# A linear-attention and Fourier-mixing kernel on one core: the k·v product with its operands' roles exchanged, more output buffers, and a new hand-written order

## The chip, the core and the metric

The kernel runs on one core of a Trainium2 chip. TensorE (PE in the profile; its weight loads are the row PEld) multiplies and transposes into PSUM, which has eight banks of 128 partitions x 512 FP32. VectorE (DVE), ScalarE (ACT) and GpSimd (POOL) do the rest, and SyncE (SP) issues the transfers between HBM and the core's own memory. Each engine takes its instructions in the order in which the program lists them, and waits at one whose input or buffer isn't ready.

The metric is the device time of one execution in microseconds (us), as the median of several runs.

## What is computed

```python
def phi(x):                                   # x: (4, 4, 1088, 32): batch, head, row, 32
    a = einsum('rd,bhsd->bhsr', S1, x)        # r = 8
    b = einsum('rd,bhsd->bhsr', S2, x)
    return einsum('bhsi,bhsj->bhsij', a, b).reshape(..., 64)

q_p, k_p = phi(q), phi(k)
kv  = einsum('bhsf,bhsd->bhfd', k_p, v)       # 64 x 32 for each batch and head
z   = sum(k_p, axis=2)
att = einsum('bhsf,bhfd->bhsd', q_p, kv) / (einsum('bhsf,bhf->bhs', q_p, z) + 1e-6)

x = att, heads side by side                   # (4, 1088, 128)
u = x + real(fft(fft(x, axis=1), axis=2))
un = (u - mean(u)) / sqrt(var(u) + 1e-6)      # over the 128 columns
out = u + relu(un @ w_ch1) @ w_ch2            # 128 -> 512 -> 128
```

So each of the four batches needs the table kv, one 64 x 32 block for each of its four heads, with z as a 33rd column, before any of its attention rows can be made. Everything behind attention needs all rows of a batch.

## The kernel before, in words

The work is written as Python generators ("chains"), one for each stage and batch. The string `ORDER` (L39 to L48) lists their names, and each name runs that chain to its next `yield`: k0 is one step of the k stage of batch 0. As nothing else schedules, `ORDER` sets the order of every engine's instructions. `BANKS` (L49 to L57) gives the PSUM bank of each accumulator in the order in which they are asked for; an accumulator waits until the bank's last reader is done.

The stages of a batch b, with their lines:

- S and T: constants (L249 to L305: `memset`s on DVE, `iota`s on POOL, ten warming matmuls), the projections `sblk` and `sab` (L310 to L313), and the tables of cosines and sines (`angles`, `turns` on DVE L226 to L235; `sines` on ACT L239, L240; tables derived from them on POOL L330 to L344). T is in two halves: a short one of 448 columns and a long one of 896.
- L: loads (L190 to L218), all issued on SP.
- k (L358): transposes of k (`ptrk`, L365), copies to `kT` (ACT, L368), projections (`pab`, L374), a copy of one factor (ACT, `ak`, L378), the products `kp` (DVE, L382), two instructions of 128x1024. Then the product with v (`pk`, L396): for each head and each of nine row tiles one FP32 matmul, and then the copies `kvt` (L404), one more matmul (`pkv`, L407) and the copies `kvz` (L411).
- v (L453): POOL copies v into `vpad` with a column of ones behind it: [v|1], 33 columns for each head.
- y and w: the ninth row tile of k and of q, which two batches share (L414 to L451).
- q (L461): transposes (`ptrq`, L468), copies `qT` (L471, L473), projections (`pq`, L483), copies `qa` (ACT, L490), products `qpT` (DVE, L497).
- p (L505): `pnd`, the product of `qpT` with `kvz` (L518), the division on DVE (`den`, `rec`, `x`, L525 to L528), then sums of x on POOL (`xw`, `xf`, L541, L543) and copies on ACT.
- z (L551): the first Fourier transform (`pz`, L558 and L565; `pze`, L573 and L577).
- D and M (`chain_u`, L591): u, the two halves of a batch; E the shared ninth tiles. Bank `pu` (L601 to L607), its copy `u` (ACT, L610), statistics (DVE, L615), five small POOL instructions, a square root (ACT, L628) and a reciprocal (DVE, L631).
- d, m and e (`chain_f`, L634): `pT` (L642 to L650), its copy `uT` (ACT, L653), four products `ph` (L658) with ReLUs to `ht`, turn about on ACT (L661) and DVE (L663), the second product `po` (L671), and on DVE `ot` = po · rstd + u (L679). SP sends `ot` out (L684; L691 in four pieces for e). For the last batch `po` and its output are cut in two.

In `pk` of before, the stationary operand is [v|1] (128 rows x 33 columns) and the moving one is `kp` (128 rows x 64 columns). Two heads, h and h+2, go to PSUM partitions 0 to 32 and 64 to 96. The result is therefore kv transposed, 33 x 64, and `pkv` turns it with an identity. There are 2 x 9 x 2 = 36 such matmuls in a batch, and each leaves two records in the profile, since an FP32 matmul runs as two passes with a weight load of its own each.

Buffers: pool `up` (L110) holds three `u` tiles and three `uT` tiles, `op` (L113) two `ot` tiles. A tile is written anew only when the last reader of the one before in its place is done; for `ot` that reader is the output transfer.

Of the kernel before, what the change touches and what calls it, by code (L numbers as in the profile page):

```python
# [10 lines left out]
FP32 = mybir.dt.float32  # L11
# [11 lines left out]
def _ap(base_ap, p0, nparts, offset_delta, dims):  # L23
    pstep = base_ap.ap[0][0]
    return bass.AP(
        tensor=base_ap.tensor,
        offset=base_ap.offset + p0 * pstep + offset_delta,
        ap=[[pstep, nparts]] + [list(d) for d in dims],
    )


def _back(ap, n):
# [4 lines left out]

WARM = [10]
ORDER = """  # L39
S T T k0 S k0 q0 k0 q0 q0 k0 y0 q0 L q0 k0 y0 v0 y0 q0 q0 k0 q0 k1 k1 L T q0 L k0 k1 k0  # L40
q1 k1 q0 q1 w0 p0 q1 q1 k1 v1 q1 p0 p0 k1 T k1 w0 p0 k2 q2 q1 w0 k2 T k1 w0 q1 q1 p0 q1
p0 v2 k2 p1 q1 k2 q2 y1 k2 W p0 q2 y1 p1 p1 y1 k2 p1 q2 p0 k2 p1 k3 k3 z0 q2 k2 w1 q2 z0
q2 p2 w1 p1 q2 k3 p1 d0 v3 q2 p2 m0 D0 w1 d0 k3 z1 d0 m0 z1 d0 d0 m0 z0 q3 z1 q2 D0 z0
m0 w1 q3 m0 q3 k3 q3 p2 D0 p2 p1 p2 q3 p2 k3 k3 q3 q3 q3 M0 q3 d0 D0 D1 e0 q3 p2 m0 e0
k3 d0 D1 E0 e0 d1 z1 D1 m1 p3 M0 p3 E0 p3 p3 M0 p2 p3 z2 z2 d1 D1 M0 z2 p3 m0 e0 d1 M1
d1 e0 m2 e0 d1 m1 E0 p3 m1 z2 d2 d1 M1 p3 m1 E0 d2 d1 d2 D2 e0 d2 m1 D2 z3 d2 M1 M2 M2
z3 D2 M1 m1 D2 z3 m1 d2 E1 M2 d2 e1 m2 z3 m2 E1 m2 M2 m2 M3 e1 e1 e1 M3 e1 m3 E1 m2 E1
m3 e1 m2 e1 m3 M3 D3 M3 d3 m3 D3 m3 d3 d3 D3 d3 d3 m3 m3 D3 m3 d3 d3 d3  # L48
"""  # L49
BANKS = [  # L50
    0, 1, 2, 3, 4, 5, 6, 7, 0, 1, 2, 3, 4, 6, 7, 0, 3, 5, 4, 1, 2, 4, 1, 5, 6, 7, 4,
    1, 5, 0, 6, 3, 2, 4, 1, 7, 6, 5, 3, 0, 2, 4, 1, 7, 6, 5, 3, 0, 1, 2, 4, 5, 3, 0,
    7, 6, 3, 0, 7, 1, 2, 4, 5, 3, 0, 7, 1, 2, 6, 4, 5, 3, 1, 2, 4, 5, 3, 1, 2, 4, 5,
    3, 1, 2, 5, 4, 3, 0, 1, 7, 2, 5, 4, 3, 6, 5, 0, 1, 4, 3, 7, 2, 6, 5, 0, 4, 1, 7,
    3, 2, 5, 0, 4, 1, 7, 3, 2, 5, 4, 0, 1, 7, 3, 6, 2, 5, 4, 1, 0, 7, 6, 2, 5, 4, 0,
    1, 7, 6, 3, 2, 5, 4, 0, 7, 1, 6, 2, 3, 4, 0, 5, 7, 1, 6, 2, 3, 4, 0, 5, 1, 7, 2,
    6, 3, 0, 4, 5, 1, 7,  # L57
]


# [1 line left out]
def kernel(  # L62
# [44 lines left out]
    qpTp = ctx.enter_context(tc.tile_pool(name="qpTp", bufs=2))  # L107
    xp = ctx.enter_context(tc.tile_pool(name="xp", bufs=2))
    zp = ctx.enter_context(tc.tile_pool(name="zp", bufs=2))
    up = ctx.enter_context(tc.tile_pool(name="up", bufs=3))  # L110
    sp = ctx.enter_context(tc.tile_pool(name="sp", bufs=4))
    hp = ctx.enter_context(tc.tile_pool(name="hp", bufs=2))
    op = ctx.enter_context(tc.tile_pool(name="op", bufs=2))  # L113
    psum = ctx.enter_context(tc.tile_pool(name="psum", bufs=1, space=bass.MemoryType.PSUM))
    banks = iter(BANKS)

    def bank(name):
        return psum.tile([128, 512], FP32, name=name, tag=f"p{next(banks)}")
# [30 lines left out]
    w1_b = const.tile([128, HID], BF16, name="w1_b")  # L149
    w2_b = const.tile([128, 4, 128], BF16, name="w2_b")  # L150
    kvz = [const.tile([128, 2, 2, D + 1], FP32, name=f"kvz{i}") for i in range(2)]
    kvts = [const.tile([128, 2, R * R], FP32, name=f"kvt{i}") for i in range(2)]
    vpads = [const.tile([128, NT, H, D + 1], FP32, name=f"vpad{i}") for i in range(2)]
    zz = [const.tile([128, 2, 512], BF16, name=f"z{i}") for i in range(2)]
    zes = [const.tile([128, 2, 128], BF16, name=f"zE{i}") for i in range(2)]
# [93 lines left out]
    def chain_start():  # L249
        nc.vector.memset(warm_act[:], 0.0)  # L250
        nc.vector.memset(wdummy[:], 0.0)
        nc.scalar.activation(out=warm_act[:, 1:2], in_=warm_act[:, 0:1], func=ACT.Sin)
        loads(0)
        make_identity(nc, ident_f[:])
        def iota(out, pattern, base, mult):
            nc.gpsimd.iota(out, pattern=pattern, base=base, channel_multiplier=mult,
                           allow_small_or_imprecise_dtypes=True)

        iota(s_f[:, 3:4], [[1, 1]], 0, 1)
        iota(kk[:, 0:DM], [[1, DM]], 0, 0)  # L260
        iota(s_f[:, 0:2], [[1, 2]], 1, 2)
        iota(kk[:, DM : DM + E], [[544, 2], [1, 32]], 256, 0)
        iota(kk[:, DM + E : DM + 320], [[1, 2], [2, 128]], 1, 0)
        nc.gpsimd.iota(odd_i[:, :], pattern=[[1, 1]], base=0, channel_multiplier=1)
        iota(s_f[0:64, 2:3], [[1, 1]], 512, 1)
        iota(s_f[64:128, 2:3], [[1, 1]], 1600, 1)
        iota(kk[:, DM + 320 :], [[1, 2], [2, 128]], 545, 0)
        for t_ in kvts:
            nc.vector.memset(t_[:], 0.0)
        for t_ in kvz:  # L270
            nc.vector.memset(t_[:], 0.0)
        nc.vector.memset(bias_halfpi[:], float(np.pi / 2))
        nc.vector.memset(bias_eps[:], 1e-6)
        nc.vector.memset(mask[:], 0.0)
        for h in range(H):
            nc.vector.memset(mask[32 * h : 32 * h + 32, h : h + 1], 1.0)
        for t_ in vpads:
            nc.vector.memset(t_[:, 0:8, :, D : D + 1], 1.0)
        for t_ in qpTes:
            nc.vector.memset(t_[:], 0.0)  # L280
        nc.vector.memset(kk[:, DM : DM + 1], 0.0)
        nc.vector.memset(kk[:, DM + 32 : DM + 33], 544.0)

        nc.vector.tensor_scalar(out=odd_i[:, :], in0=odd_i[:, :], scalar1=1, scalar2=None, op0=AND)
        nc.vector.tensor_copy(par[:, 1:2], odd_i[:, :])
        nc.vector.tensor_scalar(out=par[:, 0:1], in0=par[:, 1:2], scalar1=-1.0, scalar2=1.0,
                                op0=MULT, op1=ADD)
        nc.vector.tensor_scalar(out=s_n[:, 2:3], in0=s_f[:, 2:3], scalar1=par[:, 1:2],
                                scalar2=0.5 / S, op0=SUB, op1=MULT)
        nc.vector.memset(s_n[0:2, 2:3], 0.0)  # L290
        nc.vector.memset(s_n[64:66, 2:3], 0.5)
        for i, t_ in enumerate(vpads):
            nc.vector.tensor_copy(t_[:, 8, :, D : D + 1], _ap(par, 0, 128, i, [[0, H], [0, 1]]))
        nc.vector.tensor_scalar(out=s_n[:, 0:2], in0=s_f[:, 0:2], scalar1=1.0 / S, scalar2=None,
                                op0=MULT)
        nc.vector.tensor_scalar(out=s_n[:, 3:4], in0=s_f[:, 3:4], scalar1=1.0 / DM,
                                scalar2=None, op0=MULT)

        nc.vector.tensor_copy(_ap(sel, 0, 16, 0, [[R, R], [1, R]]),
                              _ap(ident_f, 0, 16, 0, [[1, R], [0, R]]))  # L300
        nc.vector.tensor_copy(_ap(sel, 0, 16, 64, [[R, R], [1, R]]),
                              _ap(ident_f, 0, 16, R, [[0, R], [1, R]]))
        nc.vector.tensor_copy(_ap(sel, 0, 16, 128, [[16, 4], [1, 16]]),
                              _ap(ident_f, 0, 16, 0, [[0, 4], [1, 16]]))
        keep_warm(WARM[0])  # L305
        yield


        ps12 = bank("ps12")
        nc.tensor.matmul(ps12[:, 0:192], s12[:, :, :], sel[:, :, :], start=True, stop=True)  # L310
        nc.vector.tensor_tensor(out=sblk[:, :, :], in0=_ap(ps12, 0, 128, 128, [[16, 4], [1, 16]]),
                                in1=_ap(mask, 0, 128, 0, [[1, 4], [0, 16]]), op=MULT)
        nc.scalar.copy(_ap(sab, 0, 128, 0, [[1, 128]]), ps12[:, 0:128])  # L313
        yield
# [43 lines left out]
    def chain_k(b):  # L358
# [29 lines left out]

        vpad, ep = vpads[b % 2], Y[b // 2]["ep"]
        pk = bank("pk")  # L390
        for hh in range(2):
            for t in range(NT):
                for h in (hh, hh + 2):
                    src = kp[:, h, t, :] if t < 8 else ep[:, h, :]
                    p0 = 64 * (h // 2)
                    nc.tensor.matmul(pk[p0 : p0 + D + 1, 64 * hh : 64 * hh + 64],  # L396
                                     vpad[:, t, h, :], src,
                                     start=(t == 0), stop=(t == NT - 1))
            if hh == 0:
                yield  # L400
        kvt = kvts[b % 2]
        for i in range(2):
            r = slice(64 * i, 64 * i + D + 1)
            nc.scalar.copy(kvt[r, :, :], pk[r, 0:128])  # L404
        yield
        pkv = bank("pkv")
        nc.tensor.matmul(pkv[:, 0 : 2 * (D + 1)], kvt[:, :, :],  # L407
                         _ap(ident_f, 0, 128, 0, [[64, 2], [1, D + 1]]), start=True, stop=True)
        kv = kvz[b % 2]
        for c in range(2):  # L410
            nc.scalar.copy(kv[64 * c : 64 * c + 64, :, c, :],  # L411
                           _ap(pkv, 64 * c, 64, 0, [[D + 1, 2], [1, D + 1]]))

    def last_tile(src):  # L414

# [218 lines left out]
    def chain_f(b, g):  # L634
# [13 lines left out]
        else:  # L648
            for i in range(nt):
                nc.tensor.matmul(pT[:, i * 128 : (i + 1) * 128], A[b]["x"][:, 4 * g + i, :],  # L650
                                 ident_b[:, :], start=False, stop=(i == nt - 1))
        uT = up.tile([128, 512], BF16, name="uT", tag="uT")
        nc.scalar.copy(uT[:, 0:n], _back(pT, n) if g == 1 else pT[:, 0:n])  # L653
        yield
        ht = hp.tile([128, 4, 512], BF16, name="ht", tag="ht")
# [104 lines left out]
```

## Time and profile before

| | |
|---|---|
| median of 3 runs | 91.38 us (91.29 to 91.52) |
| the profiled execution, its own time | 90.52 us |
| its span, first to last instruction | 88.7 us |
| granted TensorE clock | 0.989 |
| PE, PEld busy | 80.2 us, 63.0 us |
| DVE, ACT, POOL busy | 67.7, 62.3, 45.7 us |
| `pk` L396: matmuls, records with kp | 36 in a batch; x256 records in four batches |
| `kvt` copies L404 on ACT | x8, 2.1 us |
| `kvz` copies L411 on ACT | x8, 1.7 us |
| `memset`s of `kvt` L269 on DVE | x2, 0.3 us |
| `ot` L679 on DVE | x34, 9.6 us |

A profile comes from one execution. Its time is 1.8 us above its span, which runs from the first instruction to the last one, and 0.86 us below the median of the runs. "Busy" is the union of an engine's instructions. A matmul's record holds its way through the array as well, so records of matmuls that follow one another overlap: what one matmul costs the engine is the distance from its start to the next one's start, and not the record's length. A row of the chain of waits ("start us, us, what xcount") counts time once, so there the length divided by the number of matmuls is that distance.

### The profile page before, as it was taken

To read this page: it belongs to the slowest core of one execution; us is meant where nothing else is said; L and a number is where in the kernel's file an instruction comes from. 1 tells how busy PE (TensorE), PEld (TensorE's weight loads), DVE (VectorE), ACT (ScalarE), POOL (GpSimd) and SP (SyncE) were. 2 spreads that over 40 slices of the span, in tenths; PEclk is the share of its full clock that TensorE was granted. 3 is DMA by queue.
4 is the path that set the end of the run, shared out by engine and by line. 5 is a ranking of instruction groups with operands and counts; after the bars stand their busy time and mean duration, and the time that the engine had idled before them with its cause. 6 is when DMAs were issued, how large, how long until landed. Compare 5 with 4: busy or idle time off the path is not lost.

```text
span 88.7 us, 3662 instructions
## 1 busy us (share of the span) xinstructions
PE 80.2 (90%) x1481; PEld 63.0 (71%) x1486; DVE 67.7 (76%) x223; ACT 62.3 (70%) x160; POOL 45.7 (52%) x102
## 2 busy tenths in 40 slices
PE   4998979999999999999999999999999999798700
PEld 1366558988979589867776988978767797574500
DVE  5990599998917989419379996959979995999850
ACT  6029657576997597777999897675899967668300
POOL 7200600399242993599502629996599675443000
PEclk9999999999999999999999999999999999999995
DMA  0979888899949760000000000020030313303033
GB/s 21 289 196 277 248 224 194 224 331 282 255 62 275 198 227 0 7 0 0 7 0 0 7 0 11 16 102 7 0 118 0 120 33 124 118 0 128 24 131 106
DMA packets 15124, 9.67 MB, mean 109 GB/s; under 512 B 3972, under 2 KB 14980, under 8 KB 15108
## 3 DMA queue, kind: packets, MB, share of 16 engines
q1 hardware_dynamic: 15028, 9.44, 37.5%
q8 instruction: 11, 0.18, 0.9%
q14 instruction: 5, 0.04, 0.2%
q10 hardware_dynamic: 80, 0.01, 0.1%
HBM read 7.22 MB, written 2.23 MB: 107 GB/s over the span
## 4 chain that ended last, share of the span: by engine, by line
PE 64%; DVE 21%; ACT 4%; DMA 3%; issue 2%; SPq 1%; DVEq 0%; ACTq 0%
PE pnd L518 11%; PE pq L483 10%; PE pk L396 10%; DVE ot L679 6%; DVE ht L663 5%; PE pab L374 5%; DVE stats L615 4%; PE ptrq L468 4%; PE ptrk L365 3%; DMA out_dram<-ot 3%; PE ph L658 3%; PE pz L565 3%; PE po L671 2%; PE pT L650 2%; PE pz L558 2%
## 5 line engine op out<-in xcount | busy, mean ns | idle before, releaser
L497 DVE TENSOR_TENSOR qpT<-qa,pq 128x256 f32<-128x256 f32 x32 | 11.8, 414 | 7.1 <-ACT qa L490 7.1
L541 POOL TENSOR_TENSOR xw<-x 128x512 f32<-128x512 f32 x8 | 10.0, 1274 | 7.4 <-DVE x L528 6.5
L663 DVE TENSOR_SCALAR ht<-ph 128x512 bf16<-128x512 f32 (+1 forms) x20 | 11.5, 600 | 2.7 <-PE ph L658 2.7
L490 ACT COPY qa<-pq 128x256 f32<-128x256 f32 x32 | 9.9, 388 | 4.2 <-PE pq L483 2.2
L455 POOL COPY vpad<-vm 128x1024 f32<-128x1024 f32 x4 | 4.2, 1050 | 15.2 <-DMA vm<-in_v_dram 12.4
L382 DVE TENSOR_TENSOR kp<-ak,pab 128x1024 f32<-128x1024 f32 x8 | 9.6, 1214 | 2.9 <-ACT ak L378 2.9
L658 PE MATMUL ph<-uT,w_b 128*128 128x512 bf16 (+1 forms) x39 | 10.7, 346 | 0.5 <-ACT uT L653 0.2
L679 DVE SCALAR_TENSOR_TENSOR ot<-po,rstd,u 128x128 f32<-128x128 f32 x34 | 9.6, 341 | 1.9 <-DMA out_dram<-ot 1.0
L661 ACT ACTIVATE ht<-ph 128x512 bf16<-128x512 f32 (+1 forms) x20 | 10.5, 542 | 0.6 <-PE ph L658 0.6
L543 POOL TENSOR_TENSOR xf<-xw 128x512 bf16<-128x512 f32 x8 | 10.0, 1277 | 0.3
L671 PE MATMUL po<-w_b,ht 128*128 128x128 bf16 x136 | 9.4, 219 | 0.4 <-ACT ht L661 0.4
L518 PEld LDWEIGHTS pnd<-kvz,qpT 128*64 128x64 f32 x256 | 8.3, 137 | 1.8 <-issue 0.6
L518 PE MATMUL pnd<-kvz,qpT 128*64 128x66 f32 x256 | 9.4, 224 | 0.0
L483 PE MATMUL pq<-qT,sab 32*64 32x256 f32 x256 | 9.0, 387 | 0.0
L671 PEld LDWEIGHTS <-ht 128*128 128x128 bf16 x136 | 8.2, 98 | 1.1 <-ACT ht L661 0.5
L396 PE MATMUL pk<-kp,vpad 128*33 128x64 f32 x256 | 8.5, 219 | 0.1
L396 PEld LDWEIGHTS pk<-kp,vpad 128*33 128x33 f32 x256 | 7.6, 111 | 0.7 <-issue 0.7
L621 POOL TENSOR_TENSOR mv<-stats 128x4 f32<-128x4 f32 (+1 forms) x10 | 2.0, 202 | 11.0 <-DVE stats L615 6.3
L615 DVE BATCH_NORM_STATS2 stats<-u 128x6 f32<-128x128 f32 x34 | 7.5, 278 | 0.0
L528 DVE TENSOR_TENSOR x<-pnd,rec 128x384 f32<-128x384 f32 x12 | 6.7, 557 | 0.6
L610 ACT COPY u<-pu 128x512 f32<-128x512 f32 (+1 forms) x10 | 5.3, 526 | 2.2 <-PE pu L605 0.8
L483 PEld LDWEIGHTS pq<-qT,sab 32*64 32x64 f32 x256 | 4.9, 131 | 2.3 <-PE ptrE L418 0.8
(149 smaller groups left out, 195.3 us busy)
## 6 DMA issues: line engine op xcount, KB each, us to landing
km<-in_k_dram SPq DMA_DIRECT2D x8, 256.0 KB
qt<-in_q_dram SPq DMA_DIRECT2D x16, 128.0 KB
vm<-in_v_dram SPq DMA_DIRECT2D x4, 512.0 KB
out_dram<-ot SPq DMA_DIRECT2D x6, 256.0 KB
w_f<-in_moe_w_ch_dram SPq DMA_DIRECT2D x2, 256.0 KB
out_dram<-ot SPq DMA_DIRECT2D x4, 128.0 KB
ke<-in_k_dram SPq DMA_DIRECT2D x2, 64.0 KB
ve<-in_v_dram SPq DMA_DIRECT2D x2, 64.0 KB
```

What stands on the lines that cost most here:

```text
L396: nc.tensor.matmul(pk[p0 : p0 + D + 1, 64 * hh : 64 * hh + 64], vpad[:, t, h, :], src, start=(t == 0), stop=(t == NT - 1))
L483: nc.tensor.matmul(pq[t][64 * c : 64 * c + 64, 256 * ab : 256 * ab + 256], _ap(sab, 32 * r, 32, 64 * ab, [[1, 64]]), _ap(qT, 32 * r, 32, 5 ...
L497: nc.vector.tensor_tensor(out=_ap(qpT, 0, 128, 1024 * g + 256 * (i % 2) + i // 2, [[128, 2], [512, 2], [2, 64]]), in0=_ap(qa, 0, 128, 256 ...
L518: nc.tensor.matmul(pnd[r, o : o + 66], lhsT, kv[:, pr, :, :], start=True, stop=True)
L541: nc.gpsimd.tensor_tensor(out=xw[:, i, :, :], in0=x[:, 0:4, :], in1=x[:, 4:8, :], op=f)
L543: nc.gpsimd.tensor_tensor(out=xf[:, i, :, :], in0=xw[:, :, 0, :], in1=xw[:, :, 1, :], op=f)
L615: nc.vector.bn_stats(stats[:, i, :], u[:, i, :])
L658: nc.tensor.matmul(ph[:, 0:n], w1_b[:, 128 * c : 128 * c + 128], uT[:, 0:n], start=True, stop=True)
L661: nc.scalar.activation(out=ht[:, c, 0:n], in_=ph[:, 0:n], func=ACT.Relu)
L663: nc.vector.tensor_relu(ht[:, c, 0:n], ph[:, 0:n])
L671: nc.tensor.matmul(po[:, (i - i0) * DM : (i - i0 + 1) * DM], ht[:, c, i * 128 : (i + 1) * 128], w2_b[:, c, :], start=(c == 0), stop=(c == 3))
L679: nc.vector.scalar_tensor_tensor(out=ot[:, i, :], in0=po[:, (i - i0) * DM : (i - i0 + 1) * DM], scalar=rstd[:, i, :], in1=u[:, i, :], op0= ...
```

## The change

Four things are changed. The roles in `pk` are exchanged: `kp` (128 x 64) is stationary and [v|1] (128 x 33) moves; two heads of a pair go to partitions 0 to 63 and 64 to 127, so that kv comes out as 64 x 33 blocks, just as `pnd` wants it. The copies `kvt`, the matmul `pkv` and the two `memset`s of `kvt` are gone; `kvz` is copied straight from `pk`. The pools hold four `u` and four `ot` tiles (`uT` stays at three). And `ORDER` and `BANKS` are new from end to end.

```diff
 ORDER = """
-S T T k0 S k0 q0 k0 q0 q0 k0 y0 q0 L q0 k0 y0 v0 y0 q0 q0 k0 q0 k1 k1 L T q0 L k0 k1 k0
-q1 k1 q0 q1 w0 p0 q1 q1 k1 v1 q1 p0 p0 k1 T k1 w0 p0 k2 q2 q1 w0 k2 T k1 w0 q1 q1 p0 q1
-p0 v2 k2 p1 q1 k2 q2 y1 k2 W p0 q2 y1 p1 p1 y1 k2 p1 q2 p0 k2 p1 k3 k3 z0 q2 k2 w1 q2 z0
...
-d1 e0 m2 e0 d1 m1 E0 p3 m1 z2 d2 d1 M1 p3 m1 E0 d2 d1 d2 D2 e0 d2 m1 D2 z3 d2 M1 M2 M2
-z3 D2 M1 m1 D2 z3 m1 d2 E1 M2 d2 e1 m2 z3 m2 E1 m2 M2 m2 M3 e1 e1 e1 M3 e1 m3 E1 m2 E1
-m3 e1 m2 e1 m3 M3 D3 M3 d3 m3 D3 m3 d3 d3 D3 d3 d3 m3 m3 D3 m3 d3 d3 d3
+S T T S k0 k0 T q0 k0 q0 L q0 k0 k0 y0 v0 y0 q0 y0 T k0 k0 q0 q0 q0 k1 k1 q0 L L q1 q0
+k1 p0 q1 w0 q0 q1 k1 w0 T q1 v1 p0 k1 q1 q1 k1 w0 p0 k1 p0 q1 w0 q1 q2 p0 q1 p1 p0 q2 k2
+q1 k2 y1 q2 p1 q2 q2 p1 q2 y1 y1 p1 p0 k2 p1 p0 v2 W z0 p1 k2 z0 k3 z0 k3 k2 q3 p1 w1 k2
...
+m0 m1 E0 M1 z2 d1 z2 M1 d2 e0 p3 e0 D2 D2 m1 d2 M2 m1 d2 d2 M2 z3 M1 M1 m2 m1 z3 m1 D2
+m2 d2 m2 m2 m2 z3 d2 e1 D2 d2 z3 E1 M2 M3 e1 e1 e1 M2 E1 e1 M3 m2 E1 D3 d3 m2 m3 M3 e1
+E1 d3 D3 e1 d3 d3 D3 d3 m3 m3 D3 m3 m3 d3 d3 M3 m3 d3 m3 m3
 """
 BANKS = [
...
-    up = ctx.enter_context(tc.tile_pool(name="up", bufs=3))
+    up = ctx.enter_context(tc.tile_pool(name="up", bufs=4))
...
-    op = ctx.enter_context(tc.tile_pool(name="op", bufs=2))
+    op = ctx.enter_context(tc.tile_pool(name="op", bufs=4))
...
-    kvts = [const.tile([128, 2, R * R], FP32, name=f"kvt{i}") for i in range(2)]
...
-        for t_ in kvts:
-            nc.vector.memset(t_[:], 0.0)
...
         pk = bank("pk")
-        for hh in range(2):
+        for pr in range(2):
             for t in range(NT):
-                for h in (hh, hh + 2):
-                    src = kp[:, h, t, :] if t < 8 else ep[:, h, :]
-                    p0 = 64 * (h // 2)
-                    nc.tensor.matmul(pk[p0 : p0 + D + 1, 64 * hh : 64 * hh + 64],
-                                     vpad[:, t, h, :], src,
-                                     start=(t == 0), stop=(t == NT - 1))
-            if hh == 0:
+                for c in range(2):
+                    h = 2 * pr + c
+                    nc.tensor.matmul(
+                        pk[64 * c : 64 * c + 64, (D + 1) * pr : (D + 1) * (pr + 1)],
+                        kp[:, h, t, :] if t < 8 else ep[:, h, :], vpad[:, t, h, :],
+                        start=(t == 0), stop=(t == NT - 1))
+            if pr == 0:
                 yield
-        kvt = kvts[b % 2]
-        for i in range(2):
-            r = slice(64 * i, 64 * i + D + 1)
-            nc.scalar.copy(kvt[r, :, :], pk[r, 0:128])
-        yield
-        pkv = bank("pkv")
-        nc.tensor.matmul(pkv[:, 0 : 2 * (D + 1)], kvt[:, :, :],
-                         _ap(ident_f, 0, 128, 0, [[64, 2], [1, D + 1]]), start=True, stop=True)
         kv = kvz[b % 2]
         for c in range(2):
             nc.scalar.copy(kv[64 * c : 64 * c + 64, :, c, :],
-                           _ap(pkv, 64 * c, 64, 0, [[D + 1, 2], [1, D + 1]]))
+                           _ap(pk, 64 * c, 64, 0, [[D + 1, 2], [1, D + 1]]))
...
-        uT = up.tile([128, 512], BF16, name="uT", tag="uT")
+        uT = up.tile([128, 512], BF16, name="uT", tag="uT", bufs=3)
```

Three places where the new order differs, as the engines' instruction lists show it. On DVE, the long half of the table preparation (six instructions, L226 to L235 of before) stands ahead of the first `kp`, where it stood behind the second; its sines on ACT stand ahead of the first `kvz`. On PE, both halves of batch 0's `pk` stand ahead of the second `pq` of batch 0, where before they stood behind it and on both sides of batch 1's `ptrk`. And the last `pnd` stands earlier: after it, PE has 22.4 us of matmuls left by the distances of the rows of before, where it had 20.9.

## The prediction

> **What bounds the kernel now.** I first read the page's busy table and the 40 slices, then the busy time by stretch, the chain of waits in order of time, and each engine's timeline at both ends of the run. The page first, with each engine's share, then the chain's lines with the `pk` and `pab` of later batches:
>
> ```profile
> PE 80.2 (90%) x1481; PEld 63.0 (71%) x1486; DVE 67.7 (76%) x223; ACT 62.3 (70%) x160; POOL 45.7 (52%) x102
> ...
> PE   4998979999999999999999999999999999798700
> ```
>
> ```profile
> 16.50 0.93 PE pab L374 x32
> ...
> 50.45 2.01 PE pk L396 x72
> ```
>
> PE runs without a gap from 15 to 75 us: there a microsecond of matmuls less is a microsecond less, if the order keeps PE fed. Three places are left where PE waits: the first 15 us, a little in the middle, and the end. The early DVE and PE timelines show the first:
>
> ```profile
> 9.47 1.22 DVE L382 TENSOR_TENSOR kp<-ak,pab 128x1024 f32<-128x1024 f32 x1 [2.92 <-ACT ak L378]
> ...
> 13.91 0.38 DVE L226 TENSOR_SCALAR tx<-kk,s_n 128x320 f32<-128x320 f32 x1
> ```
>
> ```profile
> 11.58 0.34 PE L423 MATMUL pabE<-sblk,eT 128*64 128x64 f32 x4 [0.67 <-ACT eT L419]
> 11.85 1.19 PE L483 MATMUL pq<-qT,sab 32*64 32x256 f32 x32
> 13.14 1.09 PE L396 MATMUL pk<-kp,vpad 128*33 128x64 f32 x32
> ```
>
> DVE idles 2.92 us before the first `kp`, and pays 3.2 us of table work later (13.91 to 17.15), while PE waits for products. The end, on DVE's timeline and in the stretches:
>
> ```profile
> 83.32 0.58 DVE L679 SCALAR_TENSOR_TENSOR ot<-po,rstd,u 128x128 f32<-128x128 f32 x2
> 84.87 1.12 DVE L679 SCALAR_TENSOR_TENSOR ot<-po,rstd,u 128x128 f32<-128x128 f32 x4 [0.98 <-DMA out_dram<-ot]
> ```
>
> ```profile
> 75.00:80.00 5.00, 4.40 (x56) 3.39 (x55) 5.00 (x20) 3.30 (x9) 1.84 (x10) 1.00 0.19 67
> 80.00:85.00 5.00, 3.47 (x39) 2.26 (x36) 4.02 (x15) 2.44 (x6) 0.94 (x5) 1.00 0.31 106
> ```
>
> From 75 us DVE is full and PE thins out. The last four `ot` wait 0.98 us for an earlier output transfer: two buffers are too few, as the four small transfers of e1 hold SP from 79.81 to 82.26. DVE ends at 85.99, the transfer at 88.7.
>
> **The exchanged product.** The question is what a matmul with 64 stationary and 33 moving columns costs. Before, `pk` (33 stationary, 64 moving) takes 2.01 us for 36 matmuls, 55.8 ns each. `pab` (64 stationary, 64 moving, also two halves of the partitions in turn) takes 0.93 us for 16: 58.1 ns. So 31 more stationary columns with as many moving ones cost 2.3 ns. What does a weight load take? The rows of PEld:
>
> ```profile
> L518 PEld LDWEIGHTS pnd<-kvz,qpT 128*64 128x64 f32 x256 | 8.3, 137 | 1.8 <-issue 0.6 <-ACT qpTe L449 0.4 <-ACT z L569 0.4
> ...
> L396 PEld LDWEIGHTS pk<-kp,vpad 128*33 128x33 f32 x256 | 7.6, 111 | 0.7 <-issue 0.7
> ...
> L407 PEld LDWEIGHTS pkv<-ident_f,kvt 128*128 128x128 f32 x8 | 1.2, 190 | 0.1
> ```
>
> 33, 64 and 128 columns last 111, 137 and 190 ns, so 0.83 ns a column on a fixed part. On an idle array the matmul behind also shows it: the longest `pk` record is 244 ns with a median of 219 (25 more, the load), the longest `pab` record 270 with 222 (48 more). So 64 columns want about 50 ns before their matmul can begin, and a half's next load starts only 2 to 3 ns after that half's matmul before (starts of single records). Then the load alone spaces the new matmuls by over 50 ns, however few columns move. I take `pab`'s 58.1 ns, the row with the same stationary shape: 4 x 36 x (58.1 - 55.8) = **+0.3 us**. The bounds: the moving columns alone would be 55.8 x 33/64 = 28.8 ns (-3.9 us against before), a load that nothing hides 53 + 28.8 = 82 ns (+3.8 us).
>
> **What goes.** `pkv` leaves PE: 0.17 us in two of its four places in the chain, 0.37 and 0.22 in the others. I take 4 x 0.17 = **-0.7 us** (0.9 at most), all in PE's full stretch. The `kvt` copies (x8, 259 ns, 2.1 us) leave ACT. That engine idles 9.1 of the 45 us from 15 to 60, so I give it nothing more; the way from `pk` to `kvz` gets shorter, but other matmuls stand there anyway. The two `memset`s (0.28 us) stand on the opening chain, which runs DVE, ACT sines, `kT`, `pab`: that counts in the next part.
>
> **The start.** DVE's list without them reaches the table work 0.28 us sooner. `sblk` ends at 6.3, the long tables (3.24) fill DVE to 9.5, and the first `kp` waits for `ak` until 9.4 anyway. Both `kp` then end at 11.9, not 13.0, because no `qpT` stands between. `pabE` stays at about 11.5. `pk` starts at 11.65, not 13.14, and runs through to 13.7; `pq` follows. With the rows of before the first group of `pnd` ends near 18.0, with 14.7 us of matmuls issued to there; before it ended at 19.64 with 15.4. So PE has wasted 0.9 to 1.0 us less: **-0.95 us**, memsets included. Queued behind the sines (1.9 us on ACT, about 12.2 to 14.1) are `kvz`, `qa` and batch 1's `kT`, for which `pab` waits near 16.3; that fits by some tenths. POOL's tables (4.1 us) also move ahead of batch 1's `vpad`, which then ends near 19.8, when its `pk` begins. Bounds: -0.28 (the memsets alone) and -1.4.
>
> **The end.** With four `ot` tiles the 0.98 us wait goes, less a few hundredths for the pair whose `po` is just done: **-0.95 us**. Next late is `po`, whose last matmuls end at 84.1, 0.2 us behind the preceding `ot`. The fourth `u` tile takes away waits of `u` for `ot` (0.7 us in all on ACT); ACT isn't full there, so I count 0, at most -0.6.
>
> **The sum**: 0.3 - 0.7 - 0.95 - 0.95 = -2.3 us; the span becomes 86.4, the profiled time 90.52 - 2.3 = 88.2, and the median, 0.86 above that execution, **89.1**. A check on DVE: up to the last `pnd` PE has 2.1 us less to do (52.9 against 55.05 us of matmuls), so it ends at 61.1 - 2.1 - 0.95 + 0.3 = 58.4, and the last x at 60.3, as far behind as before. Behind it DVE has 21.4 us, not 20.1, since four more `ot` stand there; with 1.9 us of other idle time and 2.7 for the last transfer that gives 86.3.
>
> **Rivals.** (1) The moving columns set the pace: 28.8 ns, 4.2 us under my sum, 84.9 us. PE is the bound and the other engines have idle time for it; against it speak the 25 and 48 ns above. [...] (2) Slower: the load can't run under the stream of its own half. The place is `pk`, the price 82 ns, 3.4 us above my sum: **92.5 us**; from 74 ns on, the whole gain is gone (2.3 us / 144 = 16). For it speaks that a load starts only after the matmul before it; against it that `pab` would then need 107 ns and takes 58.1. [...] (3) The new order gives back what it saves: if batch 3's last x is no earlier than 63.0, DVE's longer queue ends the span at 63.0 + 21.4 + 1.9 + 2.7 = 89.0: 91.7 us. The point is 62.7. For it speaks that nothing in the old trace shows the new waits in the middle, against it that PE's list up to there is 2.1 us shorter.
>
> **How the numbers follow.** My forecast 0.72, rival 1 0.08, rival 2 0.05, rival 3 0.15, which lies about 91.2 to 92 and is split between faster 0.03, same 0.06 and slower 0.06. About 0.3% (0.27 us) is what a measurement here can tell from no change. Faster: 0.72 + 0.08 + 0.03 = 0.83; same 0.06; slower 0.06 + 0.05 = 0.11. The forecast's own range: all good ends together (pk at 55.8, pkv 0.9, start 1.4, u 0.6) give 87.5, the start at its bad end 89.8, and unseen waits in the middle another 0.6. The range 87.4 to 91.4 leaves out rivals 1 and 2 and half of rival 3, 0.2 in all.
>
> **What would show it.** The chain should give `pk` 36 matmuls in 2.0 to 2.1 us; 1.1 is rival 1, 2.9 rival 2. The first `pk` should start near 11.7, the first `pnd` group end near 18.0, the last x near 60.3 (63 is rival 3), and no `ot` wait for a transfer. I am wrong if one of these is off, or if DVE's idle time behind the last x exceeds 2 us.

## The result and the profile after

| | median of the runs, us | span of the profiled execution |
|---|---|---|
| before | 91.45 (91.29 to 92.0) | 88.7 |
| changed | 88.87 (88.33 to 91.25) | 87.5 |

The ratio is 0.969, with a 95% interval of 0.960 to 0.977. The forecast of 89.1 lies 0.2 us from the median. Ratios here compare undisturbed executions alone, so a ratio need not be that of the two medians beside it. The profiled execution of the changed kernel took 89.25 us; a second one of the same kernel (experiment 4) took 88.28, and where the two differ I say so.

The profile page of the changed kernel opens with the busy time of each engine:

```profile
PE 80.7 (92%) x1478; PEld 62.7 (72%) x1478; DVE 68.5 (78%) x221; ACT 59.0 (67%) x152; POOL 46.5 (53%) x102
...
PE   4999869999799999999999999999999999999920
```

ACT has lost 3.3 us, 2.1 of them the `kvt` copies; PE is as full as before from the seventh slice to the last but two, except in the eleventh (the wait at 22.53 below). The start, first on DVE's timeline, then on PE's (start, duration, engine, line, operation, tiles, shapes, count, and in brackets the idle time before and what ended it):

```profile
7.99 1.09 DVE L232 SCALAR_TENSOR_TENSOR tx<-tu,tx 128x896 f32<-128x896 f32 x1
9.12 1.34 DVE L234 TENSOR_SCALAR tu<-tx 128x896 int32<-128x896 int32 x1
10.39 2.34 DVE L379 TENSOR_TENSOR kp<-ak,pab 128x1024 f32<-128x1024 f32 x2
12.65 0.41 DVE L419 TENSOR_TENSOR ep<-ae,pabE 128x256 f32<-128x256 f32 x1
```

```profile
11.74 1.13 PE L392 MATMUL pk<-vpad,kp 128*64 128x33 f32 x32
13.20 0.31 PE L392 MATMUL pk<-vpad,ep 128*64 128x33 f32 x4 [0.34 <-POOL cd L332]
13.31 1.13 PE L392 MATMUL pk<-vpad,kp 128*64 128x33 f32 x32
14.24 0.32 PE L392 MATMUL pk<-vpad,ep 128*64 128x33 f32 x4
...
18.16 0.87 PE L507 MATMUL pnd<-kvz,qpT 128*64 128x66 f32 x23
...
22.53 0.25 PE L392 MATMUL pk<-vpad,ep 128*64 128x33 f32 x2 [0.53 <-issue]
```

DVE no longer idles before `kp`, and `pk` starts at 11.74, as expected. But it doesn't run through. The last table instruction (L234, the sign mask) takes 1.34 us where the same instruction took 0.63 before, both `kp` end at 12.7 and not at 11.9, and `pk` stands for `ep` until 13.2. (The brackets name POOL there; `ep` ends at 13.06, and is what `pk` reads next.) So the first group of `pnd`, forecast to end near 18.0, ends near 19.0. The end, in the stretch from 80 to 85 us (length, then busy time of PE, PEld, DVE, ACT and POOL) and on DVE's timeline:

```profile
80.00:85.00 5.00, 3.55 (x39) 2.31 (x36) 4.76 (x15) 2.33 (x6) 0.94 (x5) 1.00 0.32 111
```

```profile
72.16 1.27 DVE L668 SCALAR_TENSOR_TENSOR ot<-po,rstd,u 128x128 f32<-128x128 f32 x4
...
75.39 1.12 DVE L668 SCALAR_TENSOR_TENSOR ot<-po,rstd,u 128x128 f32<-128x128 f32 x4
...
83.15 1.61 DVE L668 SCALAR_TENSOR_TENSOR ot<-po,rstd,u 128x128 f32<-128x128 f32 x6
```

The last six `ot` run through with no wait for a transfer: DVE, which was busy for 4.02 us of 80 to 85, is busy for 4.76 there.

### The profile page after: what moved, and what is told of

Its sections match the earlier page's. It is cut to its first block, busy times and chain, and to the rows that moved or that the text cites. A ratio compares the mean times of both kernels' runs of the same rounds, so it can differ in the third digit from the quotient of the medians.

```text
span 87.5 us, 3634 instructions
## 1 busy us (share of the span) xinstructions
PE 80.7 (92%) x1478; PEld 62.7 (72%) x1478; DVE 68.5 (78%) x221; ACT 59.0 (67%) x152; POOL 46.5 (53%) x102
## 5 line engine op out<-in xcount | busy, mean ns | idle before, releaser
L486 DVE TENSOR_TENSOR qpT<-qa,pq 128x256 f32<-128x256 f32 x32 | 11.7, 415 | 6.8 <-ACT qa L479 6.8
L530 POOL TENSOR_TENSOR xw<-x 128x512 f32<-128x512 f32 x8 | 10.0, 1279 | 12.4 <-DVE x L517 9.3
L647 PE MATMUL ph<-uT,w_b 128*128 128x512 bf16 (+1 forms) x40 | 10.0, 347 | 0.0
L444 POOL COPY vpad<-vm 128x1024 f32<-128x1024 f32 x4 | 4.7, 1171 | 8.8 <-DMA vm<-in_v_dram 8.8
L392 PE MATMUL pk<-vpad,kp 128*64 128x33 f32 x256 | 8.9, 223 | 0.1
L392 PEld LDWEIGHTS pk<-vpad,kp 128*64 128x64 f32 x256 | 8.3, 138 | 0.7 <-issue 0.7
L642 ACT CAST uT<-pT 128x512 bf16<-128x512 f32 (+1 forms) x10 | 5.3, 542 | 1.1 <-PE pT L635 0.8
```

Of the source, the lines that this page charges most:

```text
L392: nc.tensor.matmul(pk[64 * c : 64 * c + 64, (D + 1) * pr : (D + 1) * (pr + 1)], kp[:, h, t, :] if t < 8 else ep[:, h, :], vpad[:, t, h, :] ...
L486: nc.vector.tensor_tensor(out=_ap(qpT, 0, 128, 1024 * g + 256 * (i % 2) + i // 2, [[128, 2], [512, 2], [2, 64]]), in0=_ap(qa, 0, 128, 256 ...
L530: nc.gpsimd.tensor_tensor(out=xw[:, i, :, :], in0=x[:, 0:4, :], in1=x[:, 4:8, :], op=f)
L647: nc.tensor.matmul(ph[:, 0:n], w1_b[:, 128 * c : 128 * c + 128], uT[:, 0:n], start=True, stop=True)
```

## The experiments

All kernels below ran against the old one on the same chip (median 91.53 to 91.62). The four groups of the change are taken apart first.

**1. The exchanged product alone**, in the old order without its `pkv` steps, with the old buffers:

```diff
-                    nc.tensor.matmul(pk[p0 : p0 + D + 1, 64 * hh : 64 * hh + 64],
-                                     vpad[:, t, h, :], src,
+                    nc.tensor.matmul(
+                        pk[64 * c : 64 * c + 64, (D + 1) * pr : (D + 1) * (pr + 1)],
+                        kp[:, h, t, :] if t < 8 else ep[:, h, :], vpad[:, t, h, :],
...
-        pkv = bank("pkv")
```

> The kernel before with the roles in pk exchanged and kvt, pkv and the memsets gone; old order (the eighth k step of each batch is empty), old banks without pkv's, old buffers. Theory (the load of 64 stationary columns sets the pace): 36 pk matmuls of a batch in 2.1 us, 58 ns each; PE gains 0.7 us from pkv and loses 0.3, the opening chain 0.28, so 0.4 to 0.7 us faster than before, about 90.8 us. Rival (the 33 moving columns set the pace): pk in 1.0 to 1.1 us a batch, 4 us faster, about 87.3 us.

90.05 us, ratio 0.988 (0.982 to 0.993). The last record of `pnd` starts at 60.19 in place of 60.88: 0.69 us less, and the prediction's terms for this part, the memsets of 0.28, 0.7 for `pkv` and +0.3 for `pk`, give 0.68. The times say more, 1.1 us by the ratio (0.6 to 1.6); the trace is of one execution of each kernel.

**2. The buffers alone:**

```diff
-    up = ctx.enter_context(tc.tile_pool(name="up", bufs=3))
+    up = ctx.enter_context(tc.tile_pool(name="up", bufs=4))
...
-    op = ctx.enter_context(tc.tile_pool(name="op", bufs=2))
+    op = ctx.enter_context(tc.tile_pool(name="op", bufs=4))
```

> The kernel before with four ot and four u tiles and nothing else. Theory (the end waits for an output transfer): the 0.98 us wait of the last four ot goes, about 0.95 us faster, 90.5 us, the last ot beginning near 83.9 us of the span instead of 84.87. Rival (another wait takes its place, or the order hides it): within 0.3 us of before.

88.88 us, ratio 0.975 (0.969 to 0.981): 2.3 us, more than twice the 0.95 of the prediction. DVE's timeline of the old kernel has a second place that I had not counted:

```profile
72.42 1.13 DVE L679 SCALAR_TENSOR_TENSOR ot<-po,rstd,u 128x128 f32<-128x128 f32 x4
74.48 1.13 DVE L679 SCALAR_TENSOR_TENSOR ot<-po,rstd,u 128x128 f32<-128x128 f32 x4 [0.94 <-PE ph L658]
```

The same timeline with four tiles of each:

```profile
72.42 2.16 DVE L679 SCALAR_TENSOR_TENSOR ot<-po,rstd,u 128x128 f32<-128x128 f32 x8
...
82.33 1.61 DVE L679 SCALAR_TENSOR_TENSOR ot<-po,rstd,u 128x128 f32<-128x128 f32 x6
```

The wait at 74.48 is put down to a `ph` of PE, and it goes when only buffers are added. So it was a wait for a free `ot` tile, that is for an output transfer. An `ot` doesn't even read `ph`: that should have warned me.

**3. The new order with the old product** (buffers as changed; a `pkv` step put into the new order behind each batch's second half of `pk`):

```diff
-S T T S k0 k0 T q0 k0 q0 L q0 k0 k0 y0 v0 y0 q0 y0 T k0 k0 q0 q0 q0 k1 k1 q0 L L q1 q0
+S T T S k0 k0 T q0 k0 q0 L q0 k0 k0 y0 v0 y0 q0 y0 T k0 k0 q0 q0 q0 k1 k1 q0 k0 L
```

> The kernel after with the old pk, kvt, pkv and the memsets put back; pkv's step stands up to seven names behind pk's second half and not behind the batch's first p, its bank is the one that was asked for longest ago. Theory (the exchange itself brings 0.4 to 0.7 us, the order and the buffers the rest): 0.4 to 1.0 us slower than after, 89.3 to 89.9 us. Rival (the exchange brings most of the 2.6 us): 90.5 us or more.

95.58 us, ratio 1.045 (1.038 to 1.051), far off every expectation. PE's timeline shows over half of it:

```profile
16.93 0.34 PE L407 MATMUL pkv<-ident_f,kvt 128*128 128x66 f32 x2
18.70 0.66 PE L468 MATMUL ptrq<-ident_f,qt 128*128 128x128 f32 x4 [1.44 <-ACT kvz L411]
```

The PSUM bank that I had chosen for `pkv` goes to the next step, which then waits for `kvz`'s copy. Four such waits behind `pkv`, one in each batch, add up to 3.9 us (1.44, 0.52, 0.86 and 1.05). This kernel measures my choice of banks and says nothing about the product or the order.

**4. The changed kernel again**, unaltered:

> The kernel after, unchanged, for an interval of its own and a second profile. In the first profile one table instruction on DVE (L234) took 1.34 us where it took 0.63 before, beside the copy of v on POOL, and PE stood still 0.5 us at 22 us. Theory (the copy of v and the table instruction slow each other whenever they meet): 1.2 to 1.4 us again, kp ending near 12.7 us. Rival (chance of one execution): 0.63 us, kp ending near 11.9 us. Median 88.4 to 89.2 us.

88.22 us, ratio 0.965 (0.959 to 0.970). The 0.53 us "issue" wait at 22.5 isn't there in its trace; the long L234 (1.34) and the wait of `pk` for `ep` are.

**5. Old order, exchanged product and buffers together**, the edits of 1 and 2 in one kernel:

> The kernel before with the exchanged pk and the four-deep ot and u pools, but its own old order and banks (without pkv's). Theory (the new order brings nothing of its own; the buffers bring 2.3 us and the exchange 1.1): the two gains add up, 0.962 of before, as fast as after within 0.5 us; DVE ends near 83.3 us of the span. Rival (the new order brings 0.9 us at the start, as the prediction had it): 0.5 to 1 us slower than after, 0.97 of before or more.

88.22 us, ratio 0.966 (0.961 to 0.971), which is the changed kernel's time. The new order as a whole thus adds nothing that can be measured. Each line below is the stretch between the end of the last x on DVE and DVE's own end (the third number after the comma is DVE's busy time). Before:

```profile
63.02:86.00 22.98, 19.75 (x242) 15.03 (x242) 20.51 (x73) 16.32 (x40) 12.50 (x36) 1.00 0.22 75
```

Buffers alone (experiment 2):

```profile
63.02:83.94 20.92, 19.48 (x246) 14.95 (x242) 20.36 (x74) 16.41 (x40) 12.51 (x36) 1.00 0.23 79
```

Old order with product and buffers (this experiment):

```profile
62.53:83.56 21.03, 19.56 (x245) 14.95 (x242) 20.41 (x73) 16.38 (x40) 12.56 (x36) 1.00 0.23 78
```

The changed kernel's second execution (experiment 4):

```profile
60.85:83.79 22.94, 21.63 (x270) 16.60 (x268) 21.91 (x79) 17.84 (x43) 12.55 (x36) 1.00 0.24 83
```

The buffers take DVE's idle time behind the last x from 2.47 us (22.98 - 20.51) to 0.56. The new order brings the last x 1.68 us earlier than the old one with the same parts (62.53 to 60.85), but that is no gain in itself: it leaves 1.50 us more of DVE's work behind the last x (20.41 to 21.91; 34 `ot` in place of 30), 2.07 more of PE's (19.56 to 21.63) and 0.4 more of DVE's idle time, and DVE ends 0.23 us later (83.56 and 83.79). The last x is a milestone that a reordering moves.

A fair place is one that has the same work in front of it. In both orders the same 274 matmul records, sorted differently, stand ahead of the `pq` behind the first group of `pnd`. On PE's timeline it starts here, in the old order (this experiment) and in the changed kernel (experiment 4):

```profile
19.22 1.25 PE L472 MATMUL pq<-qT,sab 32*64 32x256 f32 x32
```

```profile
19.46 1.12 PE L472 MATMUL pq<-qT,sab 32*64 32x256 f32 x32
```

The new order is 0.24 us behind there and 0.23 at DVE's end. So by these two traces the start gained nothing, and the end only shows it. Experiment 8 says why.

**6. Four `ot` tiles alone**, `u` with three:

```diff
-    op = ctx.enter_context(tc.tile_pool(name="op", bufs=2))
+    op = ctx.enter_context(tc.tile_pool(name="op", bufs=4))
```

> The kernel before with four ot tiles, and three u tiles as before. Theory (both late waits of ot, 0.94 us at 74.48 and 0.98 at 84.87, were waits for an output transfer, and that is all the buffers bring): as fast as with four of both, 0.975 of before, DVE ending near 84.0. Rival (the fourth u tile brings half, by the 0.7 us that u waited for ot): 0.985 or more, DVE ending near 85.

89.14 us, ratio 0.976 (0.972 to 0.980), against 0.975 with the fourth `u`: the `ot` tiles are nearly all of it. Its DVE idles 0.57 us behind the last x.

**7. The new order with the long tables further back**, behind both `kp`, `ep` and, on DVE, the first two `qpT`:

```diff
-S T T S k0 k0 T q0 k0 q0 L q0 k0 k0 y0 v0 y0 q0 y0 T k0 k0 q0 q0 q0 k1 k1 q0 L L q1 q0
+S T T S k0 k0 q0 k0 q0 L q0 k0 k0 y0 v0 y0 q0 y0 k0 k0 q0 T q0 q0 k1 k1 q0 T L L
```

> The kernel after with the long half of the tables moved back behind batch 0's kp, ep and first four qpT on DVE, and its sines behind batch 1's first step. Theory (moving it forward brought nothing, as its last instruction meets the copy of v on POOL and takes 1.34 us in place of 0.63): that instruction 0.63 us again, both kp ending near 11.8 in place of 12.7, the first pnd group within 0.4 us of where it is in after, the time within 0.5 us of after. Rival (the move is worth its 0.9 us): 0.7 us slower than after or more.

90.45 us, ratio 0.990 (0.986 to 0.993), 2.2 us slower than the changed kernel. The tables now stand in front of the `qpT` for which `ptrk` waits on PE:

```profile
16.95 0.65 PE L362 MATMUL ptrk<-ident_f,km 128*128 128x128 f32 x4 [1.49 <-DVE qpT L486]
```

So in this order the tables are well placed in the early gap; my idea that moving them forward brought nothing fell. A part of an order can be worth 2 us while the order as a whole is worth none. (The expectation counted four `qpT` in front of the tables; the trace has two.)

**8. The changed kernel with the sign mask (L234) alone put behind `kp` and `ep`** (`ORDER` gets one more T for it):

```diff
     def turns(c):
+        turns_a(c)
+        turns_b(c)
...
-        turns(slice(T[1], NTAB))
+        turns_a(slice(T[1], NTAB))
+        yield
+        turns_b(slice(T[1], NTAB))
```

> The kernel after, with only the last of the six long table instructions (the sign mask, L234) moved behind batch 0's kp and ep on DVE. Theory (that instruction and the copy of v on POOL slow each other, and the late kp and ep make PE wait 0.5 us at 12.6): 0.63 us for the instruction, both kp ending near 11.6, no wait of pk for ep, 0.5 to 0.8 us faster than after. Rival (PE would wait elsewhere): the pk wait goes, but the time is within 0.3 us of after.

Its DVE timeline:

```profile
9.24 2.35 DVE L386 TENSOR_TENSOR kp<-ak,pab 128x1024 f32<-128x1024 f32 x2 [0.15 <-ACT ak L382]
11.95 0.42 DVE L426 TENSOR_TENSOR ep<-ae,pabE 128x256 f32<-128x256 f32 x1 [0.36 <-ACT ae L423]
12.29 0.71 DVE L239 TENSOR_SCALAR tu<-tx 128x896 int32<-128x896 int32 x1
```

The mask takes 0.71 us there, `kp` ends at 11.6, the first `pnd` starts at 17.30 (17.96 in experiment 4), the last x ends at 60.19 (60.85), DVE ends at 83.13 (83.79), and the span is 85.9 (86.5): 0.65 to 0.66 us at every mark. The `pq` with the same work in front of it, on PE's timeline:

```profile
18.80 1.12 PE L479 MATMUL pq<-qT,sab 32*64 32x256 f32 x32
```

That is 0.42 us ahead of the old order's 19.22, and DVE's end is 0.43 ahead of the old order's 83.56. So with the mask out of the copy's way the new start does bring some 0.4 us, and all of it arrives at the end. The median, 88.11 us, ratio 0.965 (0.960 to 0.970), isn't apart from the changed kernel's or from experiment 5's. The traces, one for each kernel, show the gain; the times don't. Its median is the lowest of the complete kernels, by 0.11 us.

**9 and 10. What sets `pk`'s pace.** First, 16 moving columns in place of 33 (kv's columns 0 to 16 are left zero, so half of v is left out); second, 32 stationary features in place of 64 (the other half is left out of kv):

```diff
-                        kp[:, h, t, :] if t < 8 else ep[:, h, :], vpad[:, t, h, :],
+                        kp[:, h, t, :] if t < 8 else ep[:, h, :], vpad[:, t, h, 17:33],
```

```diff
-                        pk[64 * c : 64 * c + 64, (D + 1) * pr : (D + 1) * (pr + 1)],
-                        kp[:, h, t, :] if t < 8 else ep[:, h, :], vpad[:, t, h, :],
+                        pk[64 * c : 64 * c + 32, (D + 1) * pr : (D + 1) * (pr + 1)],
+                        kp[:, h, t, 0:32] if t < 8 else ep[:, h, 0:32], vpad[:, t, h, :],
```

> The changed kernel with 16 of v's 33 columns moving through pk in place of 33 (columns 17 to 32; the other columns of kv stay zero, so half of v is left out); the stationary 64 columns and the number of matmuls stay. Theory (the loads of 64 columns set pk's pace, 58.5 ns a matmul with 33 columns): the same pace, 58 to 59 ns, 2.1 us for 36 matmuls, and a span within 0.6 us of the changed kernel's 86.5 and 87.5. Rival (the moving columns set the pace): about 16/33 of 58.5, 28 ns, 1.0 us for 36 matmuls, about 4 us less of PE's time. Rival in between (load and stream one behind the other, 50 ns and half of the rest): about 54 ns.

> The changed kernel with 32 of the 64 features of k's products stationary in pk (the other half of the features is left out of kv), the 33 moving columns and the number of matmuls stay. Theory (the loads set pk's pace): by 0.83 ns a column, 27 ns less for 32 columns, so about 32 ns a matmul, 1.1 to 1.2 us for 36 matmuls, unless the 33 moving columns (27.5 ns by 55.8 ns for 64) then become the bound at nearly the same pace; 4 x 36 x 26 = 3.8 us less of PE's time. Rival (the moving columns or a fixed cost of each matmul set the pace): 58 ns, as before.

Each ran once (89.25 and 88.06 us). PE's timelines: the distance from the start of a group of 32 records (16 matmuls, two records each) to the start of the four that follow. With 16 moving columns:

```profile
13.26 1.12 PE L392 MATMUL pk<-vpad,kp 128*64 128x16 f32 x32
14.19 0.30 PE L392 MATMUL pk<-vpad,ep 128*64 128x16 f32 x4
```

With 32 stationary columns:

```profile
24.02 0.70 PE L392 MATMUL pk<-vpad,kp 128*32 128x33 f32 x32
24.55 0.23 PE L392 MATMUL pk<-vpad,ep 128*32 128x33 f32 x4
```

The changed kernel takes 14.24 - 13.31 = 0.93 us, 58.1 ns a matmul. Half the moving columns: 0.93 us again. Half the stationary ones: 0.53 us, 33.1 ns. So neither the moving columns nor a fixed cost of each matmul sets the pace here; the 64 stationary columns do, as the theory of the load has it. What sets the 33.1 ns, the load of 32 or the 33 moving columns, stays open.

Yet the span of the second kernel was 86.3, only 0.2 under experiment 4, with 3.6 us (144 x 25.0 ns) less for PE. Its timeline shows a stall that no engine ends:

```profile
18.79 0.98 PE L371 MATMUL pab<-sblk,kT 128*64 128x64 f32 x27 [1.71 <-issue]
```

**11. The changed kernel with two `ot` tiles:**

```diff
-    op = ctx.enter_context(tc.tile_pool(name="op", bufs=4))
+    op = ctx.enter_context(tc.tile_pool(name="op", bufs=2))
```

> The changed kernel with two out tiles in place of four, all else as changed. Theory (the tiles are worth about 2 us in the old order since four sets of ot wait for the output's transfers in the last 15 us; the new order ends with the same queue on DVE and needs them as much): ratio to before 0.985 to 1.0, 2 us slower than the changed kernel, with waits of ot for a transfer of 1 us or more each in DVE's last 15 us. Rival (the new order spreads the output's tiles, so that the end costs only the 0.98 us that the prediction took away): about 1 us slower than the changed kernel, ratio 0.975 to 0.98. Rival 2 (new order and four tiles do the same thing): within 0.5 us of the changed kernel.

91.15 us, ratio 0.980 (0.972 to 0.988). In its DVE timeline one wait comes back, the last:

```profile
85.32 1.12 DVE L668 SCALAR_TENSOR_TENSOR ot<-po,rstd,u 128x128 f32<-128x128 f32 x4 [1.57 <-DMA out_dram<-ot]
```

By the ratios it is 1.4 us slower than experiment 4, by DVE's end 1.7 us later than the first profile (86.45 against 84.76). The six executions lie between 89.25 and 92.06 us and by the medians it is 2.9 us, so the times alone leave the price open. The trace lies between the theory (2 us, several waits) and the first rival (1 us): the new order itself takes away the wait near 74, probably since its sets of `ot` stand 3.2 us apart (72.16 and 75.39 in the first profile), and leaves the last. What three `u` tiles would cost in the new order wasn't tried: the order can't run with them.

**12. Experiment 10 once more**, for the stall:

> The kernel of the run before with 32 stationary features in pk once more (half of the features left out). In that run pk fell to 33 ns a matmul, 3.7 us less for PE, but its span was 86.3, only 0.2 less than the changed kernel's: PE stood 1.9 us at 16.85 for nothing that the trace shows, and pk waited longer for ep. Theory (the stall is an accident of one execution; the first batch gains nothing, since pk waits for ep there, and the three others gain their 0.9 us each): no such stall, a span of 84.0 to 84.7, first pnd at 17.5 to 17.9. Rival (something takes the time back whenever pk is shorter): the stall is there again, or the span is 85.8 or more.

Spans of 83.4, 85.1, 86.2 and 86.5 us; the profiled one, of 86.2, has the stall again, shorter, and another:

```profile
17.34 0.98 PE L371 MATMUL pab<-sblk,kT 128*64 128x64 f32 x27 [0.34 <-issue]
...
22.85 0.25 PE L392 MATMUL pk<-vpad,ep 128*32 128x33 f32 x3 [1.11 <-issue]
```

So it isn't one execution's accident; that half of my theory fell. The shortest span, 83.4, is 2.5 us under the shortest of experiment 4 (85.9) and suggests that a shorter `pk` does pay. What the stalls probably are is told in the last section.

## Why the prediction was right, and where its terms were wrong

- **The exchanged product, +0.3: right.** A load of 64 columns sets the pace (experiments 9 and 10), at 55.3 to 58.3 ns a matmul in batches 1 to 3, where the old product has 55.2 to 57.6; the four batches of experiment 1 come to +0.2 us. The moving columns as a bound (rival 1) and a load that nothing hides (rival 2) are both excluded. (By its own 53 ns for a load, rival 2 would ask 109 ns of `pab`, not 107; nothing hangs on it.) Both halves use all 128 rows here, and 58.1 ns leave no room for the load (50 ns by the prediction's rows) and the stream of 33 columns (28.8 ns by its estimate) one behind the other.
- **`pkv` gone, -0.7: right**, by experiment 1's 0.69 us for this term, the memsets and +0.3 together; the three aren't told apart.
- **The start, -0.95: the step that failed.** (The memsets' 0.28 of it is in experiment 1 and stands; what failed is the order's 0.67.) `pk` did start at 11.7, but it didn't run through to 13.7, and the first `pnd` group ended near 18.8 and 19.0, not 18.0: by its own signs the prediction was wrong here. With the same work in front, PE is 0.24 us later than in the old order, not 0.67 earlier (experiments 5 and 4). The prediction put the long tables ahead of `kp` at the 3.24 us that they took in the old trace, 0.63 of it L234; but there the mask meets POOL's copy of v and takes 1.34, and the sum had no term for that. Moving the mask alone gives back 0.66 us, `pk` runs through, and the start is worth 0.42 (experiment 8). Why not the whole 0.67 isn't shown.
- **The end, -0.95: mis-sized.** It is -1.9 us of DVE's idle time (experiment 2), because two waits of `ot` for a tile go and not one. I read the second as a wait for `ph` since the profile named it.
- **The fourth `u`, 0: right** within what experiment 6 can tell (0.976 and 0.975).
- **The check on DVE** came near by errors that cancel as well. It put the last x at 60.3 (60.85 and 61.81; the start's gain is in it) and 21.4 + 1.9 us behind it (22.94 and 22.95): its work 0.5 too small (as was its 20.1 for the old kernel, where the stretch has 20.51), its idle time 0.9 too large.
- **Rival 3** (the new order gives back what it saves) didn't come as it was priced: the last x is 2 us ahead of 63.0, and DVE's longer queue only goes with the earlier last x. That the order brought nothing is true, but the place is the start.

In short, that 89.1 lies so near 88.87 is luck, since two errors cancelled: the buffers brought 1.0 to 1.4 us more than the 0.95 that I gave them (1.9 of idle time, 2.3 by the ratio), and the order brought nothing, not 0.67. The second measurement (experiment 4) has the gain at 3.2 us by its ratio, where the forecast had 2.3.

## What to carry to other kernels

Settle a reordering at a place that has the same work in front of it in both orders, and at the end of the queue that ends last: a milestone such as the last x comes earlier by itself when work is moved behind it. An instruction that is moved next to other engines' work can cost more there than it did (the mask took 1.34 us in place of 0.63), so look up what runs beside its new place. When a wait is put down to an engine whose result the instruction doesn't read, look for the buffer it writes to. And for short FP32 matmuls with a new stationary operand each, count the stationary columns first: here 64 cost 58 ns a matmul with 16 or with 33 moving columns, and 32 cost 33 ns.

## What was not expected of the hardware

**PE's stalls are probably late transfers of its instructions.** This is my estimate from the times below; no run changed these transfers alone. The page has a queue that it calls `instruction`, with nearly the same row in all these kernels; in the changed kernel's:

```profile
q8 instruction: 11, 0.18, 0.9%
```

That is 11 transfers of 16 KB for 2,956 records of PE and PEld. In the trace's transfer records the first of them starts 1.0 to 1.4 us after PE has passed its 182nd record in the old order (10.27 and 11.46 before; 10.04 and 11.16 in experiment 5), and ends at 12.1 to 12.4 in all five traces of that order. In the seven traces of the new order with the exchanged product and its tables first it starts 2.9 to 6.1 us after that record (2.5 in experiment 3, with the old product) and ends between 14.0 and 17.4. The transfer engines move somewhat more then (227 GB/s before and 262 to 269 in the changed kernel from 10 to 15 us). All seven such stalls of over 0.4 us (0.45 to 1.94 between starts) stand at the same three places of PE's list, behind records 435, 687 and 940, 252 or 253 apart, and end 1.3 to 1.6 us after such a transfer does (in the changed kernel at 22.53, the transfer at 21.13); five of those seven traces have one, none of the five old ones. A stall reaches the end: experiment 9, as fast as experiment 4 up to the `pq` at 19.4, has one of 0.92 us, and its DVE ends 0.97 later (84.76 and 83.79). Why the transfer starts later wasn't tried. It goes with the tables' place: with them further back (experiment 7) it starts at 11.36, 1.4 us after the 182nd record, as in the old order.

**Where DVE's sign mask and POOL's copy of v meet, the one that starts second takes longer.** L234 on 128x896 int32 takes 0.63 us where it starts ahead of POOL's copy of v (16.60 and 17.04 in the old trace) and 1.34 to 1.39 where it starts inside it. In the changed kernel it ends 0.48 us after the copy does (10.46 and 9.98), in experiments 3, 4 and 10 0.47 us after it. The copy isn't longer for it: it takes 1.04 us in experiments 9 and 12, beside a mask of 1.38 and 1.39. Its 1.54 in the changed kernel goes with the instruction before the mask, L232, which still runs until 9.08:

```profile
8.44 1.54 POOL L444 COPY vpad<-vm 128x1024 f32<-128x1024 f32 x1 [5.53 <-DMA vm<-in_v_dram]
```

Where the mask is first by a little, it is the copy that takes longer: in experiment 2 they start at 16.61 and 16.66, the mask takes 0.63 and the copy 1.47. Experiment 8 moves the mask away from the copy and it takes 0.71 (a POOL operation that it meets there, L337, takes 0.92, where the changed kernel's takes 0.53). Why the second takes longer no run shows.
